# Half of the attention's value products moved ahead of the sink transposes, and the routing gates and first gathers regrouped

## Chip, cores and metric

The kernel runs on 1 core of one Trainium2 chip. The metric is the device time of one execution in microseconds (us). Of the kernel before there are three timed runs and one profiled execution.

## What is computed

Windowed attention with sink tokens, and behind it a two-level mixture of experts. For each of 4 batches and 8 heads (768 positions, 64 values per head), a position attends to the first `n_sink` = 4 positions and to the last `window` = 128 ones; all is float32. The 3072 x 512 result is routed: first to one of 4 groups, then to one of 4 experts of the group, each by the largest logit, and each token's output is its expert's result times both softmax weights.

```
scores = where(is_sink | in_window, q @ k.T / sqrt(64), -1e9)
x = softmax(scores) @ v                                # as 3072 x 512
g = argmax(x @ w_group);  e = argmax(x @ w_expert[g])
out = softmax_g * softmax_e * (relu(x @ w1[g, e]) @ w2[g, e])
```

## The kernel before

**Attention loop.** 24 blocks of 128 positions (`NI`; 6 per batch) go through a software pipeline, one step `i` of the loop at line 1183 for each block and two more, called tail steps here (24 and 25). In a step TensorE (PE) works on four blocks, in the order of the program, which the helper at line 112 pins for every engine (so nearly all rows carry that line, and instructions are told apart by the tiles they write):

- `scores(i)`: products of queries and keys, tile `ps`, two halves of four heads. VectorE (DVE) masks them and takes the maxima (`maxima`, tile `sm`), ScalarE (ACT) takes exponentials into `pt` (`exps`).
- `trans(a)`, a = i - 1: transposes of `pt` into the PSUM pair `tp`. `evac` has ACT copy them to the two `pa` tiles; GpSimd (POOL) then masks each `pa` into a `pu` (the half block before the diagonal one) and in place, by `affine_select`, in all steps but the first of a batch.
- `logits(c)`, c = i - 3: the block's share in the routing logits, tile `lg`, from `xT`.
- `sink_t(a)`: two transposes of the sink columns `sp`, written to columns of `tp` that lie in the range the second `pa` copy reads. `sink_evac` has ACT copy them to `spT`, and `sink_rows` has POOL spread them over rows of `pu`. `sink_pack` on POOL makes the `sp` of the current block.
- `natural(c)`: transposes of `xT` into `tp`; `norm(c)` on DVE divides by the softmax sums and writes `xt`, and SyncE (SP) stores it to `xd` in DRAM.
- `values(b)`, b = i - 2 (lines 827 to 840): 32 products of `pa` (`k` = 0, the block's own values) and 32 of `pu` (`k` = 1, the block before and the sinks), all summed in the PSUM bank `po`. `out_evac` has ACT copy `po` to `xT`.

With `values` go two loads on SP's queue: `load_s(b + 1)`, the sink values, written over rows of the value tile `vv` of block b that the `k` = 0 products have read and that the `k` = 1 products of the next step read; and `load_v(i)`, the values of block i. SP issues, in a step: `qb` and `kb` of block i + 2, the store of `xt`, `load_s`, `load_v`, the gates, and now and then an expert weight `rw`.

**Routing.** Every six blocks form a batch. `route_batch` is a generator of single DVE instructions, of which each step takes a set number (`UNITS`, line 1255, and one group of PE products at line 1228). It appends six gates, one per block, to a list `gates`; `put_gates(2)` (line 1254) writes two of them per step to `xd`. When the second batch is done, `select` computes the row indices `gidx` of the first expert's first two blocks of 128 tokens and appends both to `later`. Lines 1241 and 1242 issue one gather (an indirect DMA on POOL from `xd` to `xg`) in a step, behind `sink_pack`, if `later` has one and `gates` is empty.

**Tail steps and experts.** The first tail step begins with `xpose` of the two gathered blocks: four PE transposes of `xg` each into `ph`, cast by ACT and DVE into `un`. The first expert's layer 1 then runs in slices (`ph<-un,whi` and `ph<-un,wlo`) between the last steps of attention. Its third block, (0, 2), is gathered when the third batch has been routed, in the tail. The experts follow to the end; there PE runs the products and the weights stream in from DRAM.

Of the kernel before, what the change touches and what calls it, by code (L numbers as in the profile page):

```python
# [21 lines left out]
P = 128  # L22
B, H, S, D = 4, 8, 768, 64
NT = S // P
NI = B * NT
# [13 lines left out]
NH = H * NSK  # L39
# [51 lines left out]
MAXB = 6  # L91
# [50 lines left out]
def moe_attention(tc, kqT, vN, vS, nsw, wgx, w1, w2, out):  # L142
    nc = Pinned(tc)
    v = nc.vector
    with ExitStack() as top, ExitStack() as att:
# [15 lines left out]
        def const(shape, dt, name):  # L161
            return cp.tile(shape, dt, name=name)
# [17 lines left out]
        vts, env, bat = {}, {}, {}  # L180
# [4 lines left out]
        def pair():  # L185
            return ps_p.tile([P, 2, 4 * P], F32, name="tp")

        def warm(k, dst=None):
            dst = pair()[:, 0, 0:192] if k and dst is None else dst
            for _ in range(k):  # L190
                nc.tensor.matmul(dst, wz[:, 0:P], wz, start=True, stop=True)
# [32 lines left out]
        def load_s(i):  # L224
            nc.sync.dma_start(vts[i - 1][SK].rearrange("p f n -> p (f n)"), vS[i // NT])
# [5 lines left out]
        def issue():  # L231
            if jobs:
                load(jobs.pop(0))
# [116 lines left out]
        gates = []  # L350

        def put_gates(n):
            for _ in range(min(n, len(gates))):
                t, g = gates.pop(0)
                nc.sync.dma_start(xd[t * P:(t + 1) * P, DM:XW], g)
# [116 lines left out]
        start = const([P, NE], F32, "start")  # L472
# [177 lines left out]
        xg, cg, later = {}, {}, []  # L650

        def gather(r, j):
            w = min(P, CAPT[r] - j * P)
            cc = BASE[r] + j
            if (r, j) in TWIN:
                return
            for a, b in TWIN.items():
                if b[0:2] == (r, j):
                    wait_for(f"x{a[0]}")
                    w += 32  # L660
            xg[r, j] = t = gp.tile([P, XW], F32, name="xg")
            src = xd[0:sum(BATCHES[:(SNAP if j < EC else SNAPB) + 1]) * P] if r == 0 else xd
            nc.gpsimd.indirect_dma_start(
                out=t[0:w], out_offset=None, in_=src,
                in_offset=bass.IndirectOffsetOnAxis(ap=gidx[0:w, cc:cc + 1], axis=0))
# [76 lines left out]
        def scores(i, g):  # L742
            t = i % NT
            if g == 0:
                env[i] = e = {}
                e["pt"] = wk.tile([P, H, SW], F32, name="pt", bufs=2)
                if i % 2 == 0:
                    env["st"] = wk.tile([P, 2, H], F32, name="st")
                e["st"] = env["st"][:, i % 2]
                e["sum2"] = sacc[i // 2 % 3]  # L750
                e["sum"] = e["sum2"][:, i % 2]
            m = 3 if t else 2
            for pp in range(2):
                for j, f in ((0, 0), (1, 1), (0, 1), (1, 0)):
                    d, o = slice(j * D, (j + 1) * D), slice(f * D, (f + 1) * D)
                    end = 2 + 2 * t + f
                    nc.tensor.matmul(psb[g][o, 2 * j + pp, (4 - m) * BW - D:CW], qb[d, i % NQ, 2 * g + pp, o],
                                     kb[d, 2 * g + pp, (end - m + 1) * BW - D:end * BW], start=True, stop=True)
# [34 lines left out]
        def trans(i):  # L793
            e = env[i]
            for h in range(H):
                for f in range(2):
                    r = slice(f * D, (f + 1) * D)
                    nc.tensor.transpose(env["tp"][:, f, h * D:(h + 1) * D], e["pt"][r, h, NSK:NSK + P], ident[r, r])
# [12 lines left out]
        def sink_t(i):  # L811
            for f in range(2):
                r = slice(f * D, (f + 1) * D)
                nc.tensor.transpose(env["tp"][0:D + NH, f, NDC * D:(NDC + 1) * D], spk[i % 2][r], ident[r, r])
# [9 lines left out]
        po = ob[1].rearrange("p (c n) -> p c n", c=HP)  # L824
        lg = ob[0][:, D:D + 2 * H * PW].rearrange("p (t n) -> p t n", t=2)

        def values(i):
            e = env[i]
            for k in range(2):
                rows = slice(0, P) if k == 0 else slice(0 if i % NT else D, D + NH)  # L830
                for g in range(2):
                    pk = e["pT", g][k]
                    for pl in range(2):
                        for f in range(2):
                            vk = vts[i - k][:, f]
                            for j in range(2):
                                h = 4 * g + 2 * pl + j
                                nc.tensor.matmul(po[j * D:(j + 1) * D, h // 2, f * D:(f + 1) * D], vk[rows, h * D:(h + 1) * D],
                                                 pk[rows, 2 * pl + j, f * D:(f + 1) * D],
                                                 start=k + g + pl + f == 0, stop=k + g + pl + f == 4)  # L840

        def out_evac(i):
            env[i]["xT"] = xT = wk.tile([P, NDC, P], F32, name="xT", bufs=1)
# [8 lines left out]
        def logits(i):  # L852
            xT = env[i]["xT"]
            for c in range(NDC):
                for g in range(2):
                    r = slice(g * D, (g + 1) * D)
                    nc.tensor.matmul(lg[r, i % 2, 2 * c * PW:2 * (c + 1) * PW], xT[:, c, r],
                                     wsd[:, c].rearrange("p j n -> p (j n)"), start=True, stop=True)
# [47 lines left out]
        def wait_for(key):  # L906
            while key not in ready:
                state["clk"] += 0.3
                routing(1)
# [273 lines left out]
        for i in range(NI + 2):  # L1183
            live = i < NI
            a, b, c = i - 1, i - 2, i - 3
            mid, far, old = 0 <= a < NI, 0 <= b < NI, 0 <= c < NI
            state["clk"] += 3.0
            if i == NI:
                state.update(gap=0.0, dve=state["clk"])
                sps.close()  # L1190
                put_gates(MAXB)
                while later:
                    gather(*later.pop(0))
                ps_h = fl.enter_context(tc.tile_pool(name="ps_h", bufs=4, space=PSUM, side="right", reuse_waits="tile"))
                tail.append(ps_h)
                next(ew)
                next(ew)
                if rest:
                    rest()
                    rest = None  # L1200
                if half:
                    half.pop()()()
            if live:
                scores(i, 0)
                scores(i, 1)
                issue()
                warm(FILL[i] if i < len(FILL) else 0, ob[0][:, 224:416])
            if mid or old:
                env["tp"] = pair()
            if mid:  # L1210
                trans(a)
                evac(a, 0)
                evac(a, 1)
            if old:
                logits(c)
            if mid:
                sink_t(a)
            if old:
                natural(c)
            if live:  # L1220
                maxima(i, 0)
                exps(i, 0)
                maxima(i, 1)
            else:
                next(ew, None)
            if old:
                norm(c)
            routing(1, ("pe",))
            if mid:
                sink_evac(a)  # L1230
            if live:
                exps(i, 1)
            if mid:
                sink_rows(a)
            if live:
                sink_pack(i)
            if old:
                norm_logits(c)
            if i == 0:
                late_consts()  # L1240
            if later and not gates:
                gather(*later.pop(0))
            state["clk"] += 3.0
            if far:
                values(b)
                if b + 1 < NI:
                    load_s(b + 1)
                if live:
                    load_v(i)
                out_evac(b)  # L1250
            if rest:
                rest()
                rest = None
            put_gates(2 if live else MAXB)
            routing(UNITS.get(i, REND) if live else TSTEP, (None, "rd"))
            if live and i and i % 2 == 0:
                sums(i - 1)
            if i == NI:
                sums(NI - 1)
            if live:  # L1260
                rest = half.pop()() if half else wjob()
            if i > CHOOK and (i % 2 == 0 or i > NI - 4):
                prefetch(min(RAW, len(raws) + (1 if live else RAW)))
            if not live:
                wjob()
                next(ew, None)
# [304 lines left out]
```

## Time and profile before

| | us |
|---|---|
| median of 3 runs | 525.87 |
| lowest, highest | 525.79, 526.70 |
| profiled execution, its own time | 527.13 |
| span of the profiled execution, first to last instruction | 525.4 |
| mean granted TensorE clock, share of full speed | 0.965 |

Busy is the time in which an engine runs instructions, per stretch or span. A timeline's row is a run of like instructions: its start, how long it lasted, engine, line, operation, the tile written and those read, shape, count, and in brackets the idle time ahead of it with what ended it. The next row's start less its own is what a run cost PE, since ends of matmuls are modelled and overlap the next start by some hundredths to two tenths. "issue" stands for idle time for which the profile shows no cause.

### The profile page before, as it was taken

To read this page: it belongs to the slowest core of one execution; us is meant where nothing else is said; L and a number is where in the kernel's file an instruction comes from. 1 tells how busy PE (TensorE), PEld (TensorE's weight loads), DVE (VectorE), ACT (ScalarE), POOL (GpSimd) and SP (SyncE) were. 2 spreads that over 40 slices of the span, in tenths; PEclk is the share of its full clock that TensorE was granted. 3 is DMA by queue.
4 is the path that set the end of the run, shared out by engine and by line. 5 is a ranking of instruction groups with operands and counts; after the bars stand their busy time and mean duration, and the time that the engine had idled before them with its cause. 6 is when DMAs were issued, how large, how long until landed. Compare 5 with 4: busy or idle time off the path is not lost. (4 is left out here: it accounts for less than half of the span.)

```text
span 525.4 us, 14669 instructions
## 1 busy us (share of the span) xinstructions
PE 477.2 (91%) x5419; PEld 400.8 (76%) x5419; DVE 380.6 (72%) x1178; ACT 330.2 (63%) x857; POOL 169.1 (32%) x269
## 2 busy tenths in 40 slices
PE   7788888887983939999999999999999999999994
PEld 5577777776772938888988978966896788787974
DVE  7465888898792736998784377647867797899760
ACT  3788888887792304457673376527753786788651
POOL 3465664664572200251212302302330055001301
PEclk8899999999996888999999999999999999999999
DMA  8478787888595471578287332869695995699401
GB/s 235 133 235 263 242 243 232 257 263 279 173 302 182 135 242 41 144 243 295 90 299 308 98 102 92 311 221 349 236 321 199 382 392 173 237 400 375 141 5 42
DMA packets 59873, 117.09 MB, mean 223 GB/s; under 512 B 9758, under 2 KB 22046, under 8 KB 59792
## 3 DMA queue, kind: packets, MB, share of 16 engines
q1 hardware_dynamic: 54960, 102.50, 57.7%
q0 software_dynamic: 4304, 13.26, 7.6%
q8 instruction: 45, 0.74, 0.6%
q10 hardware_dynamic: 528, 0.29, 0.3%
q14 instruction: 36, 0.29, 0.2%
HBM read 103.25 MB, written 13.24 MB: 222 GB/s over the span
## 5 line engine op out<-in xcount | busy, mean ns | idle before, releaser
L112 DVE TENSOR_TENSOR wlo<-rw,whi 128x1024 fp32r<-128x1024 f32 x112 | 134.6, 1220 | 28.5 <-ACT whi L112 28.0
L112 PE MATMUL ph<-un,whi 128*128 128x256 f32 (+4 forms) x576 | 134.8, 322 | 1.0 <-DVE cg L112 0.6
L112 PE MATMUL po<-whi,un 128*128 128x512 f32 (+2 forms) x384 | 127.5, 396 | 0.0
L112 ACT CAST whi<-rw 128x1024 fp32r<-128x1024 f32 (+1 forms) x116 | 115.4, 1017 | 10.4 <-DMA rw<-in_w 5.5
L112 POOL DMA_INDIRECT out<-ot,sidx x33 | 41.1, 1246 | 224.0 <-ACT ot L112 79.9
L112 PE MATMUL ph<-un,wlo 128*128 128x160 f32 (+4 forms) x416 | 101.8, 270 | 0.0
L112 PEld LDWEIGHTS ph<-un,whi 128*128 128x128 f32 x576 | 96.9, 195 | 3.2 <-DVE cg L112 0.9
L112 PEld LDWEIGHTS po<-whi,un 128*128 128x128 f32 (+1 forms) x384 | 70.8, 186 | 24.9 <-issue 6.7
L112 PEld LDWEIGHTS ph<-un,wlo 128*128 128x128 f32 x416 | 78.7, 193 | 0.8
L112 ACT ACTIVATE pt<-sm,st 128x136 f32<-128x136 f32 x192 | 76.1, 402 | 5.1 <-DVE st L112 4.5
L112 PE MATMUL po<-wlo,un 128*128 128x512 f32 (+3 forms) x200 | 77.5, 389 | 0.0
L112 DVE CUSTOM_DVE_ANT_0 sm<-ps,msk 128x136 f32<-128x136 f32 x192 | 45.8, 296 | 8.7 <-PE ps L112 2.2
L112 POOL DMA_INDIRECT xg<-xd,gidx x30 | 35.5, 1182 | 47.3 <-DVE idz L112 23.5
L112 PE MATMUL ps<-kb,qb 64*64 64x208 f32 (+1 forms) x768 | 42.2, 353 | 3.8 <-DMA qb<-in_kqT 1.9
L112 PEld LDWEIGHTS po<-wlo,un 128*128 128x128 f32 (+2 forms) x200 | 36.4, 182 | 7.5
L112 POOL TENSOR_SCALAR_AFFINE_SELECT pu<-pa 64x512 f32<-64x512 f32 x40 | 27.8, 694 | 42.6 <-ACT pa L112 42.6
L112 ACT COPY pa<-tp 128x512 f32<-128x512 f32 x48 | 25.8, 589 | 21.4 <-PE tp L112 21.4
L112 DVE TENSOR_TENSOR hc<-ph,hc 128x160 f32<-128x160 f32 (+2 forms) x64 | 21.8, 346 | 22.7 <-ACT hc L112 20.3
L112 ACT ACTIVATE un<-ph 128x256 fp32r<-128x256 f32 x40 | 15.4, 384 | 34.3 <-PE ph L112 31.7
L112 ACT ACTIVATION_READ_ACCUMULATOR pt<-sm,st 128x1 f32 x192 | 36.8, 192 | 0.0
L112 ACT ACTIVATE ot<-po,cg 128x512 f32<-128x512 f32 (+3 forms) x25 | 17.0, 680 | 31.0 <-PE po L112 31.0
L112 PEld LDWEIGHTS ps<-kb,qb 64*64 64x64 f32 x768 | 28.2, 141 | 10.9 <-issue 5.2
(196 smaller groups left out, 728.6 us busy)
## 6 DMA issues: line engine op xcount, KB each, us to landing
rw<-in_w SPq DMA_DIRECT2D x128, 512.0 KB
vv<-in_vN SPq DMA_DIRECT2D x24, 512.0 KB
kb<-in_kqT SPq DMA_DIRECT2D x23, 288.0 KB
qb<-in_kqT SPq DMA_DIRECT2D x24, 256.0 KB
xd<-xt SPq DMA_DIRECT2D x24, 256.0 KB
vv<-in_vS SPq DMA_DIRECT2D x24, 128.0 KB
out<-ot,sidx POOLq DMA_INDIRECT x33, 8.1
xg<-xd,gidx POOLq DMA_INDIRECT x30, 4.6
```

The source lines that it names most:

```text
L112: r = f(*a, **k)
```

## The change

`values` gets a second argument, `k`. The products of `k` = 0 stand behind `logits(c)` and ahead of `sink_t(a)`, with `load_s(b + 1)`; those of `k` = 1 stay where all were. `put_gates` takes three per step in place of two, and the gathers, now all that wait, are issued behind it in the same step, no longer ahead of the values' products.

```diff
-        def values(i):
-            e = env[i]
-            for k in range(2):
-                rows = slice(0, P) if k == 0 else slice(0 if i % NT else D, D + NH)
-                for g in range(2):
-                    pk = e["pT", g][k]
...
+        def values(i, k):
+            rows = slice(0, P) if k == 0 else slice(0 if i % NT else D, D + NH)
+            for g in range(2):
+                pk = env[i]["pT", g][k]
...
             if old:
                 logits(c)
+            if far:
+                values(b, 0)
+                if b + 1 < NI:
+                    load_s(b + 1)
             if mid:
                 sink_t(a)
...
-            if later and not gates:
-                gather(*later.pop(0))
             state["clk"] += 3.0
             if far:
-                values(b)
-                if b + 1 < NI:
-                    load_s(b + 1)
+                values(b, 1)
                 if live:
                     load_v(i)
                 out_evac(b)
...
-            put_gates(2 if live else MAXB)
+            put_gates(3 if live else MAXB)
+            while live and later and not gates:
+                gather(*later.pop(0))
```

## Rows read from the trace of the kernel before

**Rows 1.** The page's first part: busy us, share of the span, instructions.
```profile
PE 477.2 (91%) x5419; PEld 400.8 (76%) x5419; DVE 380.6 (72%) x1178; ACT 330.2 (63%) x857; POOL 169.1 (32%) x269
```

**Rows 2.** Busy time in stretches of the attention loop (steps 2 and 3, 4 to 8, 9 to 17, 18 to 23), in one step, and in two stretches of the first tail step. Columns: stretch, its length, busy us of PE, PE's weight loads, DVE, ACT and POOL (with instructions), granted clock, share of the DMA engines, GB/s.
```profile
14.24:28.98 14.74, 12.58 (x261) 9.86 (x259) 6.44 (x39) 11.95 (x51) 8.12 (x15) 0.88 0.46 135
28.98:58.74 29.76, 26.31 (x695) 22.81 (x691) 20.22 (x104) 25.93 (x103) 17.26 (x32) 1.00 0.81 253
58.74:114.43 55.69, 49.65 (x1273) 42.84 (x1269) 48.36 (x229) 46.26 (x181) 33.49 (x60) 1.00 0.80 243
114.43:157.44 43.01, 35.96 (x852) 30.06 (x849) 37.07 (x161) 35.47 (x135) 24.86 (x39) 0.96 0.79 256
34.97:40.97 6.00, 5.33 (x142) 4.60 (x138) 3.75 (x22) 5.17 (x22) 3.94 (x8) 1.00 0.83 250
162.00:168.00 6.00, 1.42 (x12) 1.12 (x14) 0.00 (x0) 0.30 (x1) 0.00 (x0) 0.50 0.57 218
168.00:174.00 6.00, 5.76 (x60) 5.18 (x58) 4.88 (x13) 2.19 (x5) 3.22 (x4) 0.50 0.13 46
```

**Rows 3.** Timeline of PE in the step from 34.97 (step 5): scores, transposes, logits, sink transposes, `natural`, the products of `pa`, those of `pu`, and the next step's scores.
```profile
34.97 1.64 PE L112 MATMUL ps<-kb,qb 64*64 64x208 f32 x32
36.54 0.71 PE L112 MATMUL tp<-ident,pt 64*128 64x64 f32 x16
37.18 0.66 PE L112 MATMUL lg<-wsd,xT 128*64 128x40 f32 x16
38.51 0.26 PE L112 MATMUL tp<-ident,sp 64*96 64x64 f32 x2 [0.67 <-ACT pa L112]
38.58 0.45 PE L112 MATMUL tp<-ident,xT 64*128 64x64 f32 x8
38.96 1.15 PE L112 MATMUL po<-pa,vv 128*64 128x64 f32 x32
39.94 1.10 PE L112 MATMUL po<-pu,vv 96*64 96x64 f32 x32
40.97 1.16 PE L112 MATMUL ps<-kb,qb 64*64 64x136 f32 x32
```

**Rows 4.** Waits of PE and of ACT from 14 to 158: who waited for whom, us in total, times, longest.
```profile
PE tp L112 <- ACT pa L112: 16.3, 23, 1.3
PE po L112 <- DMA vv<-in_vS: 0.4, 1, 0.4
...
ACT spT L112 <- DVE xt L112: 2.6, 6, 1.0
```

**Rows 5.** Timeline of PE in the tail steps: the transposes of the first and the second gathered block; the products of `pu` of step 24; the first rows of a slice of layer 1 and of the logits behind it; the last products of the routing and the transposes of block (0, 2).
```profile
157.44 0.63 PE L112 MATMUL ph<-ident,xg 128*128 128x128 f32 x4 [0.48 <-DMA xg<-xd,gidx]
166.58 1.08 PE L112 MATMUL ph<-ident,xg 128*128 128x128 f32 x4 [8.51 <-DMA xg<-xd,gidx]
...
175.04 1.10 PE L112 MATMUL po<-pu,vv 96*64 96x64 f32 x32
176.08 0.50 PE L112 MATMUL ph<-un,whi 128*128 128x256 f32 x2
...
177.68 0.67 PE L112 MATMUL lg<-wsd,xT 128*64 128x40 f32 x16
...
196.43 1.09 PE L112 MATMUL ph<-ident,xg 128*128 128x128 f32 x4 [7.89 <-DMA xg<-xd,gidx]
```

**Rows 6.** Timeline of POOL: the sink rows of step 5 behind its masks; `sink_pack` of step 21, the first mask behind it, and the two gathers.
```profile
40.69 1.16 POOL L112 COPY pu<-spT 32x512 f32<-32x512 f32 x2
...
145.68 0.21 POOL L112 COPY sp<-pt 128x32 f32<-128x32 f32 x1
146.78 0.65 POOL L112 TENSOR_SCALAR_AFFINE_SELECT pu<-pa 64x512 f32<-64x512 f32 x1 [0.89 <-ACT pa L112]
...
152.67 1.16 POOL L112 DMA_INDIRECT xg<-xd,gidx  x1 [1.01 <-DVE st L112]
...
159.30 0.97 POOL L112 DMA_INDIRECT xg<-xd,gidx  x1 [0.16 <-issue]
```

**Rows 7.** Timeline of ACT in step 5: the copies of pa, spT and xT.
```profile
37.29 1.07 ACT L112 COPY pa<-tp 128x512 f32<-128x512 f32 x2 [0.76 <-PE tp L112]
...
39.95 0.26 ACT L112 COPY spT<-tp 32x128 f32<-32x128 f32 x1
...
41.94 0.59 ACT L112 COPY xT<-po 128x512 f32<-128x512 f32 x1
```

**Rows 8.** Timeline of DVE: `norm` of step 5, and the indices of the two early gathers in step 20.
```profile
39.12 0.69 DVE L112 TENSOR_TENSOR xt<-tp,rc 128x512 f32<-128x512 f32 x1 [0.16 <-issue]
...
138.03 0.17 DVE L112 TENSOR_SCALAR gidx<-idv 128x2 uint32<-128x2 f32 x1
```

**Rows 9.** Timeline of SP's queue: the second and the third pair of gates of the second batch (steps 20 and 21).
```profile
138.29 2.16 SPq L112 DMA_DIRECT2D xd<-cw  x2
...
144.30 1.24 SPq L112 DMA_DIRECT2D xd<-cw  x2
```

More of the change, by code (lines that the diff above doesn't have):

```diff
@@ L825, in moe_attention @@
         lg = ob[0][:, D:D + 2 * H * PW].rearrange("p (t n) -> p t n", t=2)
-        def values(i):
-            e = env[i]
-            for k in range(2):
-                rows = slice(0, P) if k == 0 else slice(0 if i % NT else D, D + NH)
-                for g in range(2):
-                    pk = e["pT", g][k]
[L833 to L840, printed above, removed]
+        def values(i, k):
+            rows = slice(0, P) if k == 0 else slice(0 if i % NT else D, D + NH)
+            for g in range(2):
+                pk = env[i]["pT", g][k]
+                for pl in range(2):
+                    for f in range(2):
+                        vk = vts[i - k][:, f]
+                        for j in range(2):
+                            h = 4 * g + 2 * pl + j
+                            nc.tensor.matmul(po[j * D:(j + 1) * D, h // 2, f * D:(f + 1) * D], vk[rows, h * D:(h + 1) * D],
+                                             pk[rows, 2 * pl + j, f * D:(f + 1) * D],
+                                             start=k + g + pl + f == 0, stop=k + g + pl + f == 4)
         def out_evac(i):
```

## Prediction

> **What bounds the kernel now.** I read the page's busy shares first, then the stretches of the attention loop, one of its steps engine by engine, and last the passage from attention to experts. TensorE (PE) is busy 91% of the span and VectorE (DVE) 72% [rows 1]: the kernel as a whole is PE's, so what counts is where PE stands still or runs slow. There are two such places before the experts.
>
> First, every step of the attention loop. In the step from 34.97 to 40.97 PE works 5.33 of 6.00 us [rows 2]; its starts show one gap, 0.67 us ahead of the transposes of the sinks, which wait for ScalarE's (ACT's) copy of pa [rows 3]. The sinks' transposes write columns of the PSUM pair that this copy reads, so they stand until it is over; the products of the values write another bank and don't need it. That gap comes 23 times in the loop, 16.3 us together [rows 4].
>
> Second, the first tail step. PE transposes the first gathered block at 157.44 and the second only at 166.58, after 8.51 us of waiting for its gather [rows 5]. GpSimd (POOL) had issued the two gathers at 152.67 and 159.30, one per step [rows 6]. Behind that wait PE runs at a granted clock of 0.50, its lower level of 1.2 GHz, from 162 to 174 [rows 2]. A third wait, 7.89 us for the gather of block (0, 2), ends at 196.43 [rows 5]; nothing in the edit touches it.
>
> **Part A, half of the products into the gap.** The 32 unmasked products take 0.98 us (38.96 to 39.94) and the 32 masked ones 1.03 [rows 3]. Ahead of the sinks' transposes the first half finds PE idle for 0.67. Nothing is added: PE's own sum is 1.57 (scores) + 0.64 + 0.66 + 0.98 + 0.07 + 0.38 + 1.03 = 5.33 us [rows 3]. The sinks' transposes start 0.98 - 0.67 = 0.31 later, and `natural` with them.
>
> What is late next? *ACT*: from its first pa copy at 37.29 to the end of xT at 42.53 it runs 5.24 us nearly without a hole [rows 7], so that is its floor. The xT copy ends 0.1 us ahead of where `logits` of the next step would start (34.97 + 5.45 + 2.21 = 42.63): no stall, but no slack either. *DVE*: `norm` starts at 39.12 [rows 8], 0.1 behind the end of `natural` (39.03); natural 0.31 later puts norm's end near 40.1, and spT on ACT, at 39.95 now [rows 7], has been seen to wait for just this (2.6 us in 6 times [rows 4]). So ACT gets up to 0.25 us in a step: 5.24 + 0.25 = 5.49, against PE's 5.33; I take 5.45. *POOL*: its masks are done by 40.69 [rows 6], the moved products of the next step would start at 40.42 + 2.87 = 43.29, so they are not held.
>
> Stretch by stretch [rows 2]:
> - 14.24 to 28.98 (steps 2 and 3): ACT is busy 11.95 of 14.74, most of it in step 2; I take 1.0, between 0 and 2 x 0.98.
> - 28.98 to 58.74 (five steps): 5 x 5.45 = 27.25 against 29.76, gain 2.5; bounds 0 and 29.76 - 26.31 = 3.45.
> - 58.74 to 114.43 (nine steps): PE 49.65 and DVE 48.36 of 55.69. Two engines at such shares don't mesh without holes; I allow 0.2 us per step over PE's floor: 51.5, gain 4.2; bounds 0 and 6.0.
> - 114.43 to 157.44 (six steps, weights are cast beside them): DVE 37.07, PE 35.96, ACT 35.47 of 43.01. DVE is the fullest here, and of the 5.9 us that it idles most goes with stalls that no edit touches; I take 1.0, bounds 0 and 6 x 0.67 = 4.0.
>
> A = 1.0 + 2.5 + 4.2 + 1.0 = 8.7 us, by the bounds 0 to 15.
>
> The last of these is where a rule speaks against the edit. The Trainium skill, Perfetto Trace Analysis, section Identifying the Most-Contended Engine, says that a kernel generally improves by improving the engine with the highest occupancy; by that rule closing PE's gap would give nothing in the last stretch, and A would be 7.7. I don't follow it fully, because the rows show DVE itself idle for 5.9 us there, some of it behind PE.
>
> `load_s` goes onto SyncE's (SP's) queue some 1.5 us earlier in the step, ahead of the store of xt. It waits for the unmasked products alone, so the store, which waits for norm, isn't held by it. Once the masked products waited for this load, 0.4 us [rows 4]; I count that gain at nothing.
>
> **Part B, gates and gathers.** The six gates of the second batch go out in pairs in steps 19, 20 and 21, the last two at 138.29 and 144.30 [rows 9]. `gather` asks that no gate be left, so the gathers went out in steps 22 and 23. The indices were written at 138.03, in step 20 [rows 8]. With three per step the gates end in step 20 and both gathers stand in step 21 behind `sink_pack`, at 145.68 + 0.21 = 145.9 [rows 6]. The second, at some 147.1, is issued 12.2 us earlier than now and 10.3 us ahead of PE's transposes at 157.44: the landing that took from 159.30 to 166.58, 7.3 us, fits in. Gain 8.5 us.
>
> The clock: from 166.58 to 175.04 PE does what at the higher level takes 0.63 (transposes of one block, from the first) + 0.64 + 0.66 + 0.07 + 0.38 + 1.60 (one slice of expert layer 1, 176.08 to 177.68) + 0.98 = 4.96 us [rows 3, 5]. Without the wait up to 8.46 - 4.96 = 3.5 comes back. DVE however is busy 4.88 of 6.00 there [rows 2], so it can shorten the 8.46 by only 19%, 1.6 us. I take 2.0, near that row; bounds 0 and 3.5. B = 10.5 us, 8.5 to 12.
>
> Costs: a third gate lengthens SP's queue by 1.1 us in two steps (2.16 us for two [rows 9]), ahead of loads needed two steps later: nothing. The two gathers hold POOL for 2 x 1.16 us [rows 6] ahead of masks that stand at 146.78 and serve the following step: nothing, while that lead lasts. But a gather waits for the gates to land. The first one of before stood until 152.67, 8.4 us behind the last pair's issue at 144.30 [rows 6, 9], in a stretch of crowded queues; the same wait behind a last triple written by 138.29 + 3.2 = 141.5 ends at 149.9, holding POOL 4.0 us more. Price 0 to 4.0 us once; I take 0, since the gates stand a whole step ahead.
>
> **Sum.** A + B = 8.7 + 10.5 = 19.2 us. The profiled execution took 527.13 us (span 525.4), 1.26 over the median of 525.87; off the median: 525.87 - 19.2 = **506.7 us**. All bounds at once (A 0 to 15, B 8.5 to 12) give 499 to 517; in my own case, where neither part is wholly lost, A is 4 to 13 and the time 501 to 513.
>
> **The rivals.**
> - *DVE and ACT take the gap.* Where PE's hole closes, the other two, at 83 to 87% [rows 2], set the step; A shrinks to 3: 525.87 - 3 - 10.5 = 512.4 us. For it: the third and fourth stretches; against it: ACT's 5.24 and PE's 5.33 are both clear of 6.00. Chance 0.17.
> - *The tail gives back.* DVE's routing of the third batch sets when the index for (0, 2) is ready; if that chain moves only by the 6.0 us that DVE stands empty from 162 to 168 [rows 2], the wait that ends at 196.43 grows by the rest. B = 6: 511.2 us. Chance 0.10.
> - *It does less than it says.* If a gate or an index is left over in step 21, both gathers go out in step 22, the second at about 153.9; landed 7.3 later, at 161.2, PE still waits 3.1: 525.87 - 8.7 - 7.4 = 509.8. Chance 0.06; the rows of gates and indices speak against it.
> - *Slower: transfers pace the steps.* Place: steps 2 to 23. The loop moves 253 GB/s at a share of 0.81 [rows 2]; shorter steps ask 10% more, and the moved products read vv about 1.1 us earlier in the step. If each step then stood for its values, at 0.4 us as once for vv [rows 4], A would go from 8.7 to 0; it decides the sign only if the wait passes 0.67 + 10.5/22 = 1.15 us in every step. At 1.25, 525.87 - 10.5 + 22 x (1.25 - 0.67) = 528.1 us. Against it: 253/0.81 leaves room to some 310 GB/s. Chance 0.03. The Trainium skill, DMA: Bandwidth & Descriptors, section Latency and other measured facts, says that access to HBM goes from 0.2 us to 2 us at high load, which would push the same way; no row here separates that latency from queueing.
>
> **How the numbers follow.** My case has 0.58, the rivals 0.17, 0.10, 0.06 and 0.03, both parts at their upper bounds (under 501) 0.04, the two parts cancelling by some other stall 0.02. Range 501 to 513.5: it holds my case and the first three rivals' times, and leaves out both ends and parts of their spread, about 2 in 10. A difference of 0.2%, some 1.05 us, is what a measurement can tell. Faster 0.95, same 0.02, slower 0.03.
>
> **What would show it.** In the profile after, PE's row between logits and the sinks' transposes should be 32 products po<-pa,vv without a gap over 0.1 us, and the five steps of the second stretch should last 27 to 28 us together. Both gathers should stand next to each other on POOL in step 21, PE's two groups of four transposes of xg too, and the granted clock should be 1.00 through the first tail step. Part A is wrong if steps stay at 6.0 with a new wait on ACT or DVE in place of the old one; part B if PE still waits over 1 us for xg there, or if the wait for (0, 2) grows by over 2 us.

## The result and the profile after

The changed kernel takes 506.29 us (median of 4 runs, 504.96 to 507.69) beside 526.29 for the kernel before in the same comparison: a ratio of 0.9615 [0.9578, 0.9652]. The forecast was 506.7 us. The profiled execution took 505.47 us with a span of 503.7, 21.7 under the span before. The sum came out; its terms did not. Several of them are off, in both directions.

The page's busy shares, after:

```profile
PE 472.8 (94%) x5419; PEld 397.4 (79%) x5419; DVE 377.2 (75%) x1178; ACT 329.0 (65%) x857; POOL 168.1 (33%) x269
```

PE does the same 5419 instructions; of its 477.2 busy us [rows 1] 4.4 went, and the other 17.3 of the 21.7 are idle time. The stretches, with the columns of [rows 2]: steps 2 and 3, 4 to 8, 9 to 17, 18 to 23, then step 5 alone and the first tail step.

```profile
13.88:25.81 11.93, 11.19 (x260) 9.12 (x258) 6.45 (x39) 10.97 (x47) 7.74 (x14) 1.00 0.66 184
25.81:53.63 27.82, 26.57 (x695) 22.77 (x691) 19.14 (x102) 25.28 (x101) 17.13 (x32) 1.00 0.83 265
53.63:106.42 52.79, 50.70 (x1274) 43.21 (x1270) 46.02 (x228) 46.33 (x182) 32.90 (x60) 1.00 0.83 252
106.42:147.57 41.15, 35.30 (x853) 29.86 (x849) 36.73 (x162) 35.13 (x133) 25.91 (x40) 0.97 0.90 285
31.39:36.96 5.57, 5.35 (x143) 4.57 (x139) 4.54 (x23) 5.07 (x21) 3.94 (x8) 1.00 0.83 258
147.57:157.22 9.65, 9.11 (x157) 8.36 (x156) 8.32 (x27) 6.81 (x17) 6.80 (x11) 0.93 0.79 267
```

Against [rows 2] the four stretches gained 2.81, 1.94, 2.90 and 1.86 us. The first three come back within 0.1 us in two other profiles of these stretches (experiments 7 and 9 below). The fourth gain can't be read from one pair of profiles: steps 18 to 23 of the loop of before took 43.01 us here, but 40.69, 41.17 and 44.50 in experiments 4, 8 and 12, which leave those steps as they are, and the changed kernel took 41.15 and, in experiment 7, 40.12. From the first tail step to the transposes of block (0, 2) it was 38.99 us before [rows 5] and is 28.14 now, a gain of 10.85. What is left, 0.36 ahead of step 2 and 0.98 behind block (0, 2), makes the 21.7.

PE in step 5, to be read against [rows 3]:

```profile
31.39 1.64 PE L112 MATMUL ps<-kb,qb 64*64 64x208 f32 x32
32.96 0.71 PE L112 MATMUL tp<-ident,pt 64*128 64x64 f32 x16
33.89 0.67 PE L112 MATMUL lg<-wsd,xT 128*64 128x40 f32 x16 [0.22 <-ACT xT L112]
34.38 1.13 PE L112 MATMUL po<-pa,vv 128*64 128x64 f32 x32
35.44 0.26 PE L112 MATMUL tp<-ident,sp 64*96 64x64 f32 x2
35.53 0.41 PE L112 MATMUL tp<-ident,xT 64*128 64x64 f32 x8
35.88 1.15 PE L112 MATMUL po<-pu,vv 96*64 96x64 f32 x32
```

The gap of 0.67 us is gone and the 32 unmasked products stand in it. In its place stands a new wait, 0.22 us, ahead of the logits. The waits of PE and of ACT through the loop (who for whom, us in total, times, longest):

```profile
ACT spT L112 <- DVE xt L112: 12.4, 19, 1.9
PE lg L112 <- ACT xT L112: 4.3, 15, 0.3
...
PE po L112 <- DMA vv<-in_vS: 2.0, 3, 1.0
PE tp L112 <- POOL sp L112: 1.8, 1, 1.8
PE tp L112 <- ACT pa L112: 1.4, 2, 1.3
```

Of 16.3 us behind ACT's pa [rows 4] 1.4 is left. ACT's wait for `norm` grew from 2.6 us in 6 times to 12.4 in 19. That is not ACT's harm alone: it closes a loop. ACT's copies from the spT of step 4 to the spT of step 5, and DVE's `norm` of step 5:

```profile
31.27 0.26 ACT L112 COPY spT<-tp 32x128 f32<-32x128 f32 x1 [0.47 <-DVE xt L112]
...
33.25 0.59 ACT L112 COPY xT<-po 128x512 f32<-128x512 f32 x1
...
36.83 0.26 ACT L112 COPY spT<-tp 32x128 f32<-32x128 f32 x1 [0.45 <-DVE xt L112]
```

```profile
36.05 0.69 DVE L112 TENSOR_TENSOR xt<-tp,rc 128x512 f32<-128x512 f32 x1 [0.45 <-ACT pt L112]
```

Follow it: spT at 31.27, four exponentials, xT at 33.25, PE's logits at 33.89, the moved products at 34.38, sinks at 35.44, `natural` at 35.53, `norm` at 36.05, spT again at 36.83. (The row of `norm` names ACT's exponentials as what ended its wait; but it starts 0.1 us behind the end of `natural`, 35.94, just as in the kernel before, 39.03 and 39.12 [rows 3, 8], so I take `natural` for it.) The round takes 5.56 us, and so does the step. No engine is full in it (PE 5.35, ACT 5.07 of 5.57); the moved products' 1.06 us lie on it.

The tail. POOL in steps 21 and 22, then PE from the unmasked products of step 23 on:

```profile
135.53 1.17 POOL L112 DMA_INDIRECT xg<-xd,gidx  x1 [0.98 <-DMA vv<-in_vS]
137.00 0.96 POOL L112 DMA_INDIRECT xg<-xd,gidx  x1 [0.31 <-issue]
...
143.22 1.16 POOL L112 COPY pu<-spT 32x512 f32<-32x512 f32 x2 [2.52 <-ACT pt L112]
144.45 0.21 POOL L112 COPY sp<-pt 128x32 f32<-128x32 f32 x1
```

```profile
141.74 1.13 PE L112 MATMUL po<-pa,vv 128*64 128x64 f32 x32
144.71 0.26 PE L112 MATMUL tp<-ident,sp 64*96 64x64 f32 x2 [1.84 <-POOL sp L112]
...
145.66 1.98 PE L112 MATMUL po<-pu,vv 96*64 96x64 f32 x32
147.57 1.70 PE L112 MATMUL ph<-ident,xg 128*128 128x128 f32 x8
...
175.71 1.09 PE L112 MATMUL ph<-ident,xg 128*128 128x128 f32 x4 [8.10 <-DMA xg<-xd,gidx]
```

Both gathers went out in step 21, and PE's eight transposes of xg need no wait, where it stood 8.51 us [rows 5]. But POOL's first copy of sink rows behind them stood 2.52 us, and the pack behind that copy (the copy to sp, 144.45) made PE stand 1.84 us at the sinks; the products right behind ran at the lower clock (1.98 us against 1.10, granted clock 0.50 from 145.66 to 147.57). The row names ACT, but spT, which this copy reads, was written by 138.9; in the built program a wait for both gathers' landing stands right ahead of the copy, and in experiment 9 below the row names it. The program of the kernel before has that wait too, for its first gather. There it cost nothing: the gather, issued at 152.67, had landed when PE read its rows at 157.44 [rows 5, 6], and the copy followed the masks without a stand at 157.67.

### The profile page after: what moved, and what is told of

Read it like the earlier page. It is cut to its first block, busy times and chain, and to the rows that moved or that the text cites. A ratio compares the mean times of both kernels' runs of the same rounds, so it can differ in the third digit from the quotient of the medians.

```text
span 503.7 us, 14681 instructions
## 1 busy us (share of the span) xinstructions
PE 472.8 (94%) x5419; PEld 397.4 (79%) x5419; DVE 377.2 (75%) x1178; ACT 329.0 (65%) x857; POOL 168.1 (33%) x269
## 5 line engine op out<-in xcount | busy, mean ns | idle before, releaser
L112 PE MATMUL ph<-un,whi 128*128 128x256 f32 (+4 forms) x576 | 132.9, 319 | 1.3 <-DVE un L112 0.8
L112 POOL DMA_INDIRECT out<-ot,sidx x33 | 43.0, 1302 | 225.8 <-ACT ot L112 87.7
L112 PEld LDWEIGHTS ph<-un,whi 128*128 128x128 f32 x576 | 95.3, 191 | 3.3 <-DVE un L112 1.0
L112 POOL DMA_INDIRECT xg<-xd,gidx x30 | 32.7, 1092 | 45.2 <-DVE idz L112 22.9
L112 PE MATMUL ps<-kb,qb 64*64 64x208 f32 (+1 forms) x768 | 38.9, 339 | 2.3 <-DMA qb<-in_kqT 1.8
L112 POOL COPY pu<-spT 32x512 f32<-32x512 f32 x48 | 29.7, 645 | 21.2 <-ACT spT L112 17.8
```

What stands on the lines that cost most here:

```text
L112: r = f(*a, **k)
```

## The experiments

Each ratio is to the kernel before, timed on the same chip in the same comparison. The first four kernels shared one comparison, the next four another, the last four a third.

**The parts alone.** Experiment 1 is the changed kernel with the gates and gathers of before:

```diff
+            if later and not gates:
+                gather(*later.pop(0))
             state["clk"] += 3.0
...
-            put_gates(3 if live else MAXB)
-            while live and later and not gates:
-                gather(*later.pop(0))
+            put_gates(2 if live else MAXB)
```

> The kernel after with gates and gathers as before (two gates per step, one gather per step, ahead of the masked products): part A alone. Theory (the two parts add, A as summed, 8.7 us; the trace of after gives 9.9 for the loop's stretches): 516 to 518 us, and PE still waits 7 to 9 us for the second gathered block in the first tail step. Rival (ACT and DVE take the gap, A = 3): 523 us. Rival (the parts don't add, because the saved time of the loop comes back in the wait for the second gather, whose landing is fixed by something other than the loop): over 520 us with a wait above 10 us.

Measured: 515.3 us, 0.9767 [0.9723, 0.9812], a little under the theory's 516 to 518: the split is worth 12.3 us [9.9, 14.6] (10.6 between the two profiled spans, 525.4 and 514.8), where the prediction had 8.7. Its stretches, the last from the second xg transposes to block (0, 2):

```profile
14.15:26.11 11.96, 11.20 (x261) 9.11 (x259) 6.44 (x39) 11.00 (x47) 7.75 (x14) 1.00 0.57 166
26.11:53.98 27.87, 26.61 (x695) 22.80 (x691) 19.15 (x102) 25.32 (x101) 17.14 (x32) 1.00 0.81 264
53.98:107.55 53.57, 50.71 (x1274) 43.01 (x1270) 46.41 (x228) 46.48 (x182) 32.80 (x60) 1.00 0.82 249
107.55:148.29 40.74, 36.19 (x853) 29.99 (x849) 36.22 (x159) 34.34 (x128) 24.56 (x40) 0.96 0.86 274
...
157.28:185.63 28.35, 20.01 (x301) 18.41 (x301) 16.27 (x45) 7.76 (x15) 5.37 (x7) 0.86 0.54 175
```

Gains against [rows 2, 5]: 2.78, 1.89, 2.12 and 2.27 in the loop (the last within the spread named above), and 1.50 in the last row (196.43 - 166.58 = 29.85 before). This 1.50 is not the gap, of which the tail had 0.24 us. It is the clock: from the second transposes to the products of `pu` of step 24 it took 6.43 us at a mean granted clock of 0.71, where it had been 8.46 at 0.52, and 0.5 of that was lost again later. The wait for the second gather stayed (8.34 us).

Experiment 2 is the kernel before with three gates per step and both gathers behind them, the products as they were:

```diff
-            if later and not gates:
-                gather(*later.pop(0))
...
-            put_gates(2 if live else MAXB)
+            put_gates(3 if live else MAXB)
+            while live and later and not gates:
+                gather(*later.pop(0))
```

> The kernel before with only the second part: three gates per step, both gathers behind them in one step. Theory: B = 10.5 us, so 515 to 517 us, no wait for gathered blocks at the start of the tail, granted clock 1.00 there; steps 4 to 17 of the loop as before (6.0 us). The built program has POOL's first copy of sink rows behind a gather wait until the gathers have landed; if that is what made PE wait 1.84 us for POOL in step 23 of after, a wait of PE for sp shows here as well, if smaller, as the steps are longer. Rival (the tail gives back): 520 us or more, with the later wait for block (0, 2) above 10 us.

Measured: 520.5 us, 0.9879 [0.9827, 0.9931]: 6.4 us [3.6, 9.1], under the 10.5 of the prediction. The tail itself gave what was forecast: 160.12 to 189.02, 28.90 us against 38.99, and the wait ahead of block (0, 2) was 8.24, so nothing was handed on. What was lost came before it: steps 18 to 23 took 44.22 us (40.69 to 44.50 in the four profiles of the loop of before), with this in them:

```profile
155.93 0.34 PE L112 MATMUL tp<-ident,sp 64*96 64x64 f32 x2 [2.06 <-POOL sp L112]
...
160.12 1.09 PE L112 MATMUL ph<-ident,xg 128*128 128x128 f32 x8
```

The same stand as in the changed kernel. The profiled execution also spent 16.21 us in steps 2 and 3 (14.74 before), which no edit touches and which I can't put down to the change. On top of the split the gathers were worth some 8 us by the two ratios, 0.9767 and 0.9615, give or take 3; the two kernels were not timed in one comparison.

**The stand on POOL, and the loop.** Experiment 3 changes two orders in the changed kernel:

```diff
-            if mid:
-                sink_evac(a)
             if live:
                 exps(i, 1)
             if mid:
-                sink_rows(a)
+                sink_evac(a)
             if live:
                 sink_pack(i)
+            if mid:
+                sink_rows(a)
```

> The kernel after with ACT's copy spT put behind the second half of the exponentials, and on POOL the packing of the current sinks ahead of the spreading of the former ones; no work added or removed. Theory (the step of 5.56 us is one loop: xT copy, logits, unmasked products, sink transposes, natural, norm on DVE, spT, second exponentials, xT copy; ACT stands 0.45 us per step for norm): the loop is cut, steps 4 to 8 take 5.33 to 5.40 each, and the whole is 2 to 4 us faster than after, 502 to 504 us. Rival (ACT's own work is the floor, the wait of 0.45 only shows slack): steps stay at 5.5 and the time within 1 us of after, 505 to 507.

Measured: 502.87 us, 0.9558 [0.9512, 0.9605]. Steps 4 and 5 took 5.30 us each, but step 6 took 6.41, so that the five steps of the second stretch were only 0.1 us shorter than in the changed kernel (27.71); PE had no wait for sp. To tell the two orders apart, each swap was run by itself, beside the changed kernel. Experiment 5, POOL's order alone:

```diff
             if live:
                 exps(i, 1)
+                sink_pack(i)
             if mid:
                 sink_rows(a)
-            if live:
-                sink_pack(i)
```

> The changed kernel with one swap on POOL: sink_pack of the new block ahead of sink_rows of the block before; ACT's order is that of the changed kernel. Theory (the stand in the last step of the loop is POOL's: its first copy behind the two gathers holds the pack that PE's sink transposes want): PE's wait of 1.84 us for sp is gone, its masked products behind run at the higher clock, the steps elsewhere stay at 5.5 to 5.6 us, total 2 to 3 us under the changed kernel (503 to 504.5). Rival (the loop through ACT's copy of spT is what the earlier run with both orders swapped won on): the total stays within 1 us of the changed kernel, though the 1.84 us wait is gone, since something else stands there.

Experiment 6, ACT's order alone:

```diff
-            if mid:
-                sink_evac(a)
             if live:
                 exps(i, 1)
             if mid:
+                sink_evac(a)
                 sink_rows(a)
```

> The changed kernel with one swap on ACT: the second half of the exponentials ahead of the copy of spT; POOL's order is that of the changed kernel. Theory (a loop norm, spT, exponentials, xT, logits, unmasked products, natural paces the step at 5.56 us): steps 4 and 5 take 5.3 us, the wait of ACT for DVE's xt falls from 12.4 us to under 5, the total is 1 to 4 us under the changed kernel (502 to 505), PE's wait of 1.84 us for sp stays. Rival (POOL's pack alone makes the difference): steps stay at 5.5 us, total within 1 us of the changed kernel.

Experiment 7 is the changed kernel, unedited:

> The changed kernel itself, beside the three others on the same chip. Every theory: 505 to 508 us, 0.958 to 0.965 of the kernel before, steps of 5.5 to 5.6 us in the second stretch.

Measured: the changed kernel 506.12 us (505.10 to 506.46), 0.9600 [0.9560, 0.9639]; POOL's order 504.01 (503.28 to 506.35), 0.9574 [0.9530, 0.9618]; ACT's order 504.23 (502.30 to 506.20), 0.9553 [0.9512, 0.9595]. Each is some 2 us under the changed kernel by the medians; the intervals against the kernel before overlap, so the sizes are rough. The traces tell the two apart. With POOL's order the pack goes ahead of the copy that waits, and PE no longer stands:

```profile
139.41 0.21 POOL L112 COPY sp<-pt 128x32 f32<-128x32 f32 x1 [0.57 <-ACT pt L112]
140.06 1.16 POOL L112 COPY pu<-spT 32x512 f32<-32x512 f32 x2 [0.44 <-DMA xg<-xd,gidx]
```

```profile
141.59 0.26 PE L112 MATMUL tp<-ident,sp 64*96 64x64 f32 x2
...
142.53 1.15 PE L112 MATMUL po<-pu,vv 96*64 96x64 f32 x32
143.61 1.09 PE L112 MATMUL ph<-ident,xg 128*128 128x128 f32 x8
```

Products and transposes run at full rate here (1.15 and 1.09 us, not 1.98 and 1.70): without the stand the lower clock did not come either. In the unedited repeat the stand was 0.91 us and the granted clock behind it 1.00, so the loss varies from one execution to the next. With ACT's order it stays (3.30 us for sp), but ACT's wait for `norm` is nearly gone and the steps are shorter:

```profile
ACT spT L112 <- DVE xt L112: 2.3, 1, 2.3
```

```profile
26.06 1.64 PE L112 MATMUL ps<-kb,qb 64*64 64x208 f32 x32
...
31.34 1.64 PE L112 MATMUL ps<-kb,qb 64*64 64x208 f32 x32
...
36.64 1.16 PE L112 MATMUL ps<-kb,qb 64*64 64x136 f32 x32
```

5.28 and 5.30 us a step against 5.57, and PE is busy through all 10.58 us of the two: the loop read above did pace the step, and taking the exponentials out of it (they go ahead of spT's copy) shortens it. Steps 4 to 8 took 26.85 us (26.06 to 52.91) and steps 9 to 17 51.75 (to 104.66), 0.97 and 1.04 less than in the changed kernel. Both theories hold, each for its own part. Experiment 3, with both orders, has the lowest median, but its ratio can't be told from those of experiments 5 and 6.

**Is it the pair of gathers?** Experiment 9 lets one gather out per step in the changed kernel:

```diff
-            while live and later and not gates:
+            if live and later and not gates:
                 gather(*later.pop(0))
```

> The changed kernel, but only one of the two early gathers may go out in a step: the first in step 21, the second in step 22, behind the pack of block 22. Theory (the stand of PE for POOL's pack, 1.84 and 0.91 us in two profiles, comes of POOL's first copy waiting for the landing of two gathers, and the second lands last): the wait for sp in step 22 is under 0.5 us, but the second gather goes out some 7 us later (near 144) and lands near 150, so that PE waits 1 to 4 us for xg in the first tail step; total 0 to 3 us over the changed kernel (506 to 509). Rival (the pair is what costs, and the second has time enough): no wait for xg, total 1 to 2 us under the changed kernel (504 to 505).

Measured: 505.92 us, 0.9585 [0.9546, 0.9623], no different from the changed kernel. Of the theory neither expectation of the trace came true (POOL, then PE), and of the rival only the missing wait for xg:

```profile
135.80 1.16 POOL L112 DMA_INDIRECT xg<-xd,gidx  x1 [0.99 <-DMA vv<-in_vS]
143.25 1.16 POOL L112 COPY pu<-spT 32x512 f32<-32x512 f32 x2 [3.55 <-DMA xg<-xd,gidx]
...
144.84 0.97 POOL L112 DMA_INDIRECT xg<-xd,gidx  x1 [0.15 <-issue]
```

```profile
144.74 0.26 PE L112 MATMUL tp<-ident,sp 64*96 64x64 f32 x2 [1.60 <-POOL sp L112]
...
147.35 2.23 PE L112 MATMUL ph<-ident,xg 128*128 128x128 f32 x8
```

One gather alone holds POOL just as long (here the row names it), PE stood 1.60 us for sp, and the second, issued at 144.84, made no wait among the eight transposes from 147.35. The landing of one gather is enough to hold POOL. Experiment 11 has experiment 3's orders and one gather per step:

> The changed kernel with POOL's pack ahead of its sink rows, ACT's exponentials ahead of the copy of spT, and one early gather per step. If the swap on POOL has already taken the hold away, a gather per step has nothing left to give and only makes the second one later: 503 to 506 us, with a wait for xg of 0 to 3 us. If landing of two gathers still holds POOL's sink rows (1.69 us in the profile with both swaps), it gives up to 1 us: 501.5 to 503.

Measured: 505.87 us (500.77 to 506.18), 0.9576 [0.9532, 0.9619]: no better than experiment 3. PE waited 1.56 us for the second gather, as the first branch had it.

**What the clock behind the wait costs.** Experiments 4 and 8 are the kernel before with products of zeros between the two groups of xg transposes, 60 and 100 of them:

```diff
                 next(ew)
+                warm(60, spare()[:, 0:192])
                 next(ew)
```

> The kernel before with 60 added products of zeros (128 x 192, bf16) between the transposes of the first and the second gathered block, so that PE is busy through most of the 8.51 us of waiting; everything else as before. It prices the clock alone. Theory (the clock's part of B is 2.0 us, between 1.6 and 3.5): the wait stays, the granted clock is 1.00 behind it and the time 522.5 to 524.7 us. Rival (DVE sets that stretch, so PE's clock is worth nothing): 526 us, same as before.

> The kernel before with 100 products of zeros between the transposes of the first and of the second gathered block, so that PE works through nearly all of the 8.5 us that it stood there; they write a PSUM tile that nothing reads, and nothing of the result changes. With 60 of them PE still stood 3.48 us, and the clock fell once more behind it. Theory of the prediction (2.0 us of what the wait costs is the clock behind it, bounds 0 and 3.5): 522.5 to 524.5 us, granted clock 1.00 in the 6 us behind the wait. Rival (the work behind waits for DVE and the queue, whatever the clock): 525 to 526.5 us with the clock at 1.00. Rival (the products push the second transposes back): the transposes start over 0.5 us later than the gather lands, and the total is that much above the first figure.

Measured: 525.46 us, 0.9963 [0.9930, 0.9995] with 60; 525.92, 0.9955 [0.9924, 0.9987] with 100, which is 2.4 us [0.7, 4.0] in the second comparison. With 60, PE ended its filling at 161.1 and still stood 3.48 us:

```profile
158.00:164.00 6.00, 3.09 (x38) 2.86 (x35) 0.13 (x2) 0.00 (x0) 0.68 (x1) 1.00 0.86 308
164.00:170.00 6.00, 5.19 (x52) 4.51 (x53) 3.00 (x6) 2.13 (x4) 2.51 (x3) 0.53 0.01 4
```

The clock fell behind what was left, so this one priced only a part. With 100 the wait is filled:

```profile
157.22 8.41 PE L112 MATMUL ph<-wz 128*128 128x192 bf16 x100
165.47 0.60 PE L112 MATMUL ph<-ident,xg 128*128 128x128 f32 x4
...
171.36 1.10 PE L112 MATMUL po<-pu,vv 96*64 96x64 f32 x32
```

From the second transposes to the products of `pu` it is 5.89 us against 8.46 [rows 5], at a granted clock of 1.00. That is 2.6 us of clock, or 30% of the 8.46; the prediction took 2.0 from bounds of 0 and 3.5, since DVE seemed to allow only 19%. The total of 525.92 taken alone lies in the second rival's range, but the kernel before took 528.07 in this comparison, and with the stretch 2.6 us shorter that rival is out. The third is not seen: PE read the rows 7.09 us after the gather's issue at 158.38, against 7.28 before [rows 5, 6].

**The clock in steps 2 and 3.** Experiment 12 is the kernel before with 13 such products in step 2's gap:

```diff
                 evac(a, 1)
+            if i == 2:
+                warm(13, ob[0][:, 224:416])
             if old:
                 logits(c)
```

> The kernel before with 13 products of zeros in step 2, ahead of the sinks' transposes, in the 1.26 us where PE stood for ACT's copy of pa; nothing reads them. Theory (of the 2.8 us that the changed kernel gained in steps 2 and 3, some 1.4 to 1.8 come from the clock: the scores of step 3 took 3.05 us at the lower level and take 1.64): the granted clock stays at 1.00 from 14 to 29, steps 2 and 3 last 13.0 to 13.5 us instead of 14.74, total 1 to 2 us under the kernel before. Rival (the gain is the products' move alone, or the clock at the start varies between executions): steps 2 and 3 last 14.2 us or more, or the total is within 0.7 us of the kernel before.

Measured: 526.13 us, 0.9975 [0.9942, 1.0007]. The stretch does what the theory says:

```profile
12.89:25.92 13.03, 12.17 (x272) 10.24 (x272) 6.79 (x43) 11.83 (x50) 8.13 (x15) 1.00 0.58 176
```

The scores of step 3, which take 1.64 us here, were this row in the kernel before:

```profile
21.57 3.05 PE L112 MATMUL ps<-kb,qb 64*64 64x208 f32 x32
```

13.03 us at 1.00, against 14.74 at 0.88 [rows 2]: 1.7 us of clock, with the time of the gaps of before still in it. The start does vary between executions, as the rival says, but not that far down: without the added products the same two steps took 14.76, 14.73 and 16.21 us in experiments 4, 8 and 2. On the total it is not resolved. In the profiled execution the lead was gone by the first tail step (157.48 against 157.44), so it shows what the clock costs the stretch and not what that is worth at the end.

**The load of the sinks' values.** Experiment 10 puts it back behind the masked products:

```diff
                 values(b, 0)
-                if b + 1 < NI:
-                    load_s(b + 1)
...
                 values(b, 1)
+                if b + 1 < NI:
+                    load_s(b + 1)
```

> The changed kernel with the load of the sinks' values back behind the masked products, where the kernel before had it. Theory of the prediction (its place costs and gives nothing): within 0.5 us of the changed kernel (505.5 to 506.7). Rival (the earlier issue is needed now, since the masked products waited for this load 2.0 us in 3 times even so): the wait of PE for vv from the sinks' values is over 4 us in the loop, total 2 to 6 us over the changed kernel.

Measured: 507.22 us, 0.9619 [0.9585, 0.9653]; the repeat of the changed kernel, in another comparison, had 0.9600 [0.9560, 0.9639]. Its one profiled execution took 512.17 us, 4 us more than the longest of the other six, and isn't read. The rival's 2 to 6 us are not seen, though the intervals leave room for its lower end; whether the load's place costs nothing or about 1 us stays open.

## Why the prediction was right, and where its steps were not

The mechanisms were right: the gap closed, the wait for the second gather went, nothing was handed on to block (0, 2) (8.10 us against 7.89). The sizes, in us, from one profile of each kernel:

| term | predicted | split alone | changed kernel |
|---|---|---|---|
| A, steps 2 and 3 | 1.0 | 2.78 | 2.81 |
| A, steps 4 to 8 | 2.5 | 1.89 | 1.94 |
| A, steps 9 to 17 | 4.2 | 2.12 | 2.90 |
| A, steps 18 to 23 | 1.0 | 2.27 | 1.86 |
| first tail step to (0, 2) | 10.5 (B) | 1.65 | 10.85 |

- *Steps 2 and 3* were mis-sized, beyond the upper bound of 1.96, because only the gap was counted. The scores of step 3 took 3.05 us behind that gap in the kernel before and take 1.64 now; experiment 12 puts the clock at 1.7 of the 2.8.
- *Steps 4 to 17.* The text named what is late next, ACT's copy of spT behind `norm`, and priced it as up to 0.25 us added to ACT's own 5.24. It is a loop over three engines instead (ACT, PE, DVE), 5.56 us long. The prediction's own numbers hold its sign: it let xT end at 42.53, 0.1 ahead of the next logits at 42.63, and then put spT, which stands ahead of xT on ACT, up to 0.25 later; with that xT ends at 42.78, and the logits wait. That step failed by 0.6 us over five steps and by 1.3 to 2.1 over nine. Experiment 6 shows it: one order on ACT gives 5.3 in most steps, and gains of 2.91 and 3.94 over the two stretches, near the 2.5 and 4.2 of the prediction.
- *Steps 18 to 23.* By the rule quoted from the Trainium skill (Perfetto Trace Analysis, Identifying the Most-Contended Engine) they should have gained nothing, since DVE is the fullest there. The pairs of profiles show 1.86 and, with the split alone, 2.27; but the loop of before took from 40.69 to 44.50 us here in four profiles, and the changed kernel 40.12 and 41.15 in two. So whether the rule or the 1.0 us of the prediction is nearer stays open.
- *The tail* is 10.85 in the place of 10.5, but 1.65 of it is the split's, most of it the clock in the first tail step, which the prediction left out. The clock term (2.0) measured 2.6 in the trace of experiment 8; DVE, which was to hold it at 1.6, did not set that stretch.
- *"I take 0, since the gates stand a whole step ahead"* is the step of B that failed. Ahead of the first gather POOL stood only 0.98 us. But it was held all the same, at its first copy behind, by the landing; the prediction had the size (0 to 4.0) and the victim, POOL, and not this mechanism. It cost PE 0.91 and 1.84 us in two profiles and, behind the 1.84, the clock: 0.93 in the first tail step, where 1.00 was foreseen.

So by the medians A is 12.3 us [9.9, 14.6] and not 8.7, and B 6.4 [3.6, 9.1] alone, or some 8, give or take 3, behind A, where 10.5 was foreseen. The errors have opposite signs; that the forecast of 506.7 came within 0.4 us of the 506.29 is luck in good part. Of the rivals, *DVE and ACT take the gap* would have made A 3, which experiment 1 excludes, though its loop is real; *the tail gives back* and *it does less than it says* did not come, by the rows of block (0, 2) and of the gathers. Of *transfers pace the steps* there is a trace: the DMA share in steps 18 to 23 rose from 0.79 (0.86 and 0.82 in experiments 4 and 8) to 0.90, and the masked products stood for the sinks' values 2.0 us in 3 times, once 0.4 before.

## What to carry to other kernels

When a gap on the fullest engine is closed, look for the closed round through the other engines that the step must still make, and add up its latencies: it can pace the step while every engine shows idle time. When an indirect DMA is issued earlier, ask which instruction stands next on the issuing engine and whether it waits for the landing; put whatever another engine needs ahead of it. A sum that comes out is no proof of its terms: run the parts alone, and look at a stretch in several profiles before reading a gain off one pair.

## What the runs showed of the hardware

A wait that was filled in part did not keep the clock: with 60 products and 3.48 us left empty the granted clock behind was 0.53, with 100 and nothing left it was 1.00 (experiments 4 and 8). In experiment 9 the landing of a single gather held POOL's next copy of sink rows for 3.55 us, until 7.4 us after the issue at 135.80, with the DMA engines at a share of 1.00 in between; the one issued at 144.84, at the loop's end, was read by the eight transposes that began at 147.35 with no wait recorded.
